# Normalised activations of the second row quarter: from a TensorE transpose to a DMA transpose, with a new instruction order

## The chip, the cores and the metric

The kernel runs on one core of a Trainium2 chip. The metric is the device time of one execution in microseconds (us). TensorE (PE) multiplies matrices, VectorE (DVE), ScalarE (ACT) and GpSimd (POOL) work on elements, SyncE (SP) mostly issues DMAs. DMAs stand in two queues here, one that SP feeds and one that ACT feeds; both are served by the same 16 DMA engines.

## The reference, cut to what matters

```python
xn = layernorm(A_q)                       # 2048 x 512
# branch A: a 4-tap shift, a long causal convolution by FFT, two gates
k_shift = sum over t of k_pad[:, t:t+S] * shift_k[:, 3-t]
kv = k_shift * v
y  = irfft(rfft(kv padded) * rfft(ssm_k padded)) + kv * ssm_D
s  = xn * y
# branch B: a gated MLP on the same normalised rows
h  = gelu(xn @ w_gate) * (xn @ w_up)      # 512 -> 1792, twice
g  = silu(h @ w_down)                     # 1792 -> 512
return A_q + s * g
```

## The kernel before, in words

**Branch B.** The 2048 rows are worked in four quarters q of 512 rows (four tiles of 128). For a quarter, `ln(q)` (L805) normalises rows of `X` into `XN` on DVE with one POOL instruction for the power of -1/2. `xn_transpose(q)` (L828) turns the four 128x512 tiles of `XN` into `xnT`, whose buffer has two halves, used by even and odd quarters. Then 14 calls of `unit(q, m)` (L1060) make the gate and up products of 128 columns each (4 matmuls `xnT,Wg` and 4 `xnT,Wu` of 128x512), gelu on ACT (`GE`) and the product on DVE (`HT`). `down(q)` (L1094) multiplies `HT` by `Wd`, 14 matmuls for each of four row tiles.

**Branch A.** The convolution is done as a two-stage transform by matrix products. The filter (`Hn`) is transposed on TensorE (L865) and goes through stage 1 (`HTr,F`), its results are stored to DRAM as `ZH` (8 stores from ACT's queue) and read back as `BH` for stage 2. The shifted and gated input (`kshift(i)`, L939, nine DVE instructions of 128x2048 for each quarter, written into `V`) goes through stage 1 (`V,F`, L900): for each u of 0 to 7 two products, each copied by ACT or DVE into a half of an `AST` or `ASX` slot, and then one SP store `ZK`. The `ZK` rows are read back as `BK`, multiplied by the filter's spectrum, transformed back (`ZI`, `BI`) and gated at the end.

**The four transposes before.** For quarters 0 and 1, `xn_transpose` puts 16 TensorE transposes of 128x128 (L841, in four groups of four) into PSUM banks and four copies to `xnT` (L846). For quarters 2 and 3 one DMA issued by SP (L833) transposes all 128x2048 elements from SBUF to SBUF; it stands in SP's queue with a length of 6.7 us in the plan.

**What sets the order.** `Sched.add` only records tasks. `Sched.run` (L344) walks the list `SEQ` (L27), a written-out order of all tasks by number (a `b` takes the task's second engine), gives each its engine and its buffers, and keeps a planned time for each from constants at L295 to L303. The instructions are then emitted in exactly this order, so each engine's stream, and each DMA queue, is the part of `SEQ` that falls to it, and each engine works its stream strictly in order. The planned times decide only which buffer slot a task takes. Loads of inputs are planned on an engine of their own name, "loads", but are issued by SP: on the chip they and SP's other DMAs are one stream. An instruction waits for semaphores: SP, too, stops at a DMA whose data is not ready, and everything behind it in its stream stops with it.

The plan charges a load its time in the table `LOAD_NS` and a fixed 2450 ns to land; a store that leaves before 46 us takes `TAKEN` from the loads:

```python
            if eng == "loads":
                free[eng] = t.start + dur * (self.EARLY[1] if t.start < self.EARLY[0] else 1.0)
                t.end = free[eng] + self.LOAD_LAT
            elif t.nbytes:
                en = t.end
                if en < self.SHARED:
                    free["loads"] += self.TAKEN
```

Of the kernel before, what the change touches and what calls it, by code (L numbers as in the profile page):

```python
# [19 lines left out]
NQ = 4  # L20
# [4 lines left out]
N_WARM = 14  # L25
ORDER = "x00 x01 w0 w1 h0 h1 h2 h3 D0 w2 s0 k0 v0 x1 w3 k1 v1 d0 d1 k2 v2 k3 v3 x2 x3"
SEQ = (  # L27
    "2 16 17 7 3 0 10 8 4 1 6 5 11 65 67 22 9 66 68 23 49 73 74 69 70 75 76 48 82 12 83 71 51 72 77 78 86b 53 55b 80 79 18 19 25 20 35 30 21 24 29 31 "
    "87 36 33 32 110 124 52 369 50 111 371 125 14 370 131 85 361 84 362 61 363 88b 364 372 89 132 60 373 112 365 375 113 37 63 62 367 374 366 13 447 "
    "449 451 445 450 446 368 452 448 376 453 454 15 457 455 377 133 381 134 383 379 54 385 378 389 139 141 138 140 391 57 382 380 384 456 59 56 126 "  # L30
    "390 386 387 58 127 392 458 95 96 388 97 421 98 413 135 114 142 415 115 460 414 143 144 422 27 28 26 38 34 423 416 405 128 459 424 145 146 150 64 "
    "147 99 136 137 129 393 461 395 462 401 409 394 465 130 463 407 464 466 411 116 396 403 148 410 402 105 412 397 119 151 404 152 107 106 417 418 "
    "419 117 420 108 118 495 406 121 120 122 153 408 154 149 398 471 90 497 399 91 92 491 93 492 100 493 101 102 400 155 494 499 496 217 42 40 158 "
    "473 94 501 109 218 103 500 425 467 39 44 45 43 41 156 498 159 502 472 219 474 160 157 511 222 475 123 104 469 220 221 476 161 513 477 223 478 "
    "162 224 435 232 436 225 233 468 234 227 235 228 437 229 479 426 163 166 164 167 470 168 165 169 230 481 438 427 430 431 440 441 242 428 81 432 "
    "429 170 171 439 226 182 172 47 244 231 174 236 177 46 176 243 237 433 245 442 483 238 173 239 484 485 240 443 486 487 246 175 241 489 252 253 "
    "254 512 434 444 634 514 247 249 480 255 515 248 256 636 482 635 250 178 516 517 179 251 507 508 503 180 543 638 640 637 639 641 518 642 643 547 "
    "509 187 183 184 544 545 646 645 644 546 510 548 504 519 185 521 505 181 257 647 520 488 490 188 189 190 549 538 539 523 258 550 283 259 270 186 "
    "192 506 551 522 262 524 528 525 552 271 526 272 556 554 553 260 555 261 263 275b 533 529 284 285 534 273 264 288b 527 535 648 265 191 266 296 "
    "530 540 531 268b 274 193 536 669 532 715 537 541 267 269 286 276 671 194 670 542 653 665 195 655 649 666 672 277 278 287 651 289 667 281 279 650 "  # L40
    "654 290 656 661 291 657 557 197 663 292 652 294b 668 658 297 610 298 301b 711 659 612 611 198 309 196 199 207 202 662 586 613 562 200 310 293 "
    "564 314 280 311 707 664 299 660 201 322 300 302 719 558 594 563 596 560 303 565 587 595 203 588 597 589 204 578 598 304 205b 580 305 559 579 590 "
    "581 312 561 307 600 206 323 582 282 592 308 306 327 324b 295 599 602 601 313 603 315 208 584 604 566 209 583 591 316 325 210 317 585 568 318 320 "
    "326 605 348 335 212 211 606 328 574 329 593 575 330 570 576 567 577 331b 569 333 336 571 337b 673 572 608 340 573 338 339 334 675 321 341 689 "
    "342 213 607 674 624 214 215 691 343 216 344 346 609 676 625 701 690 349 703 692 319 350 351 352 353 614 332 345 347 615 702 354 616 355 697 617 "
    "699 356 704 357 359b 358 619 626 698 360 627 705 713 700 618 620 629 709 681 621 622 683 682 623 628 684 677 693 630 631 679 678 706 680 723 708 "
    "770 742 714 685 632 695 687 694 710 732 729 725 716 696 712 733 686 735 633 734 774 772 736 730 721 688 743 722 717 731 724 778 727 744 718 737 "
    "726 745 738 746 720 728 749 750 780 751 756 752 747 776 757 739 753 758 775 773 763 740 759 764 754 765 760 761 766 779 771 748 781 777 741 767 "
    "755 768 762 769 "
)  # L50
NF_BANKS = 4
ISSUE = 470.0
# [239 lines left out]
class Sched:  # L292
# [7 lines left out]
    SHARE_BW = 300.0  # L300
    FIRST = {"loads": 300.0, "SP": 30500.0}
    DRAIN = 121.0
    EARLY, TAKEN, SHARED, WAIT = (2500.0, 1.6), 1700.0, 46000.0, 3300.0  # L303

    def __init__(self):
        self.tasks = []
# [87 lines left out]
def build_kernel(nc, A_q, A_k, A_v, A_shift_k, A_ssm_k, A_ssm_D, B_w_gate, B_w_up, B_w_down, out):  # L394
    with ExitStack() as es0:
# [20 lines left out]
        XN = new("XN", [128, NT, DM], BF16)  # L416
# [8 lines left out]
        ident = new("ident", [128, 128], BF16)  # L425
# [67 lines left out]
        S = Sched()  # L493
# [11 lines left out]
        def bank16(b):  # L505
            return PSB[:, 1024 * b.slot:1024 * (b.slot + 1)]

        def R_bank(b):
            return [R_ps[b.slot // 2][b.slot % 2]]
# [83 lines left out]
        def copy(e, h, o, i, scale=1.0):  # L593
            if e == "ACT":
                return h.activation(o, i, ACTF.Copy, scale=scale)  # L595
            if scale != 1.0:
                return h.tensor_scalar(o, i, scale, None, ALU.mult)
            return h.tensor_copy(o, i)
# [11 lines left out]
        bS = [B(f"S{j}") for j in range(8)]  # L610
        bst = [B(f"st{t}") for t in range(NT)]
        bmv = [[B(f"mv{q}_{h}") for h in range(2)] for q in range(NQ)]
        bxnT = [[B(f"xnT{q}_{h}") for h in range(1 if q > 1 else 4)] for q in range(NQ)]
        bF1, bG1, bMF, bMI, bid, bSKB = B("F1"), B("G1"), B("TF"), [B(f"MI{i}") for i in range(2)], B("id"), [B(f"SKB{j}") for j in range(4)]
        bHT = [[B(f"HT{q}_{m}") for m in range(MF)] for q in range(NQ)]
        bW = {n: [B(f"{n}{i}") for i in range(4)] for n in ("g", "u")}
# [188 lines left out]
        def ln(q):  # L805
            t_pws = []
            for t in range(4 * q, 4 * q + 4):
                t_stats[t] = op([("DVE", 670.0)], lambda e, h, t=t: h.bn_stats(stats[:, t, :], X[:, t, :]), r=[bX[q][t % 4]], w=[bst[t]], rr=[R_X[t]], ww=[R_st[t]])  # L808
                op([("DVE", 170.0)], lambda e, h, t=t: h.bn_aggr(mv[:, t, 0:2], stats[:, t, :]), r=[bst[t]], w=[bmv[q][t % 4 // 2]], rr=[R_st[t]], ww=[R_mv[t]])
            for h in range(1 if q else 2):  # L810
                n = 4 if q else 2
                ts = slice(4 * q + 2 * h, 4 * q + 2 * h + n)
                rm = R_mv[ts]
                bm = bmv[q] if q else [bmv[q][h]]
                be, b = B(f"var{q}_{h}"), B(f"rstd{q}_{h}")
                t_var = op([("DVE", 180.0)], lambda e, hd, ts=ts: hd.tensor_scalar(mv[:, ts, 2:3], mv[:, ts, 1:2], LN_EPS, None, ALU.add), r=bm, w=[be], rr=rm, ww=rm)  # L816
                t_pw = op([("POOL", 850.0)], lambda e, hd, ts=ts, n=n: hd.tensor_tensor(mv[:, ts, 3:4], mv[:, ts, 2:3], NHALF[:, 0:n, :], ALU.pow),  # L817
                          r=[bconst, be] + bm, w=[b], rr=rm + [R_nh], ww=rm)
                for t in range(ts.start, ts.stop):
                    op([("DVE", 420.0)], lambda e, hd, t=t: hd.tensor_scalar(XN[:, t, :], X[:, t, :], mv[:, t, 0:1], mv[:, t, 3:4], ALU.subtract, ALU.mult),  # L820
                       r=[bX[q][t % 4], b], w=[bXN[t]], rr=[R_X[t], R_mv[t]], ww=[R_XN[t]])
                t_pws.extend([t_var, t_pw])
            return t_pws

# [2 lines left out]

        def xn_transpose(q):  # L828
            af = gu_tasks[q - 2] if q >= 2 else (skb if q else [])
            if q > 1:  # L830
                def f(e):
                    o = xnT[:, q % 2, :, :, :].rearrange("k j d p -> k (j d) p")
                    trk.dma(e, lambda h: h.dma_start(out=o, in_=XN[:, 4 * q:4 * q + 4, :].rearrange("p t d -> p (t d)"), transpose=True), d_xt, r=R_XN[4 * q:4 * q + 4], w=R_xnT[q % 2])  # L833
                S.add([("SP", 6700.0)], f, r=bXN[4 * q:4 * q + 4], w=bxnT[q], nbytes=W_XT, after=af)
                return
            pp = [B(f"psxn{q}_{j}", pX) for j in range(4)]
            for j in range(4):
                def tr(e, j=j):
                    for kd in range(KD):
                        o = bank16(pp[j])[:, 128 * kd:128 * (kd + 1)]  # L840
                        trk.op("PE", lambda h, o=o, kd=kd: h.transpose(o, XN[:, 4 * q + j, 128 * kd:128 * (kd + 1)], ident[:]), r=[R_XN[4 * q + j], R_id], w=R_bank(pp[j]), accum=True)  # L841
                S.add([("PE", 4 * 66.0)], tr, r=[bid, bXN[4 * q + j]], w=[pp[j]], lat=200.0)
            for j in range(4):
                def ev(e, h, j=j):
                    return copy(e, h, xnT[:, q, j, :, :].rearrange("p k c -> p (k c)"), bank16(pp[j])[:, 0:512])
                xnT_tasks.append(op([("ACT", act(512)), ("DVE", dve(512, 2))], ev, r=[pp[j]], w=[bxnT[q][j]],  # L846
                   rr=lambda j=j: R_bank(pp[j]), ww=[R_xnT[q][j]], after=af))

        d_out = []
        gu_tasks = [[] for _ in range(NQ)]  # L850
# [387 lines left out]
```

## Time and profile before

| what | before |
|---|---|
| time, median of 3 (lowest to highest) | 196.93 us (196.27 to 197.09) |
| the profiled execution: its time, its span | 197.06 us, 195.3 us |
| around the span in that execution (the difference) | 1.8 us |
| granted TensorE clock | 1.000 |
| TensorE matmuls with 128x512 outputs on the whole array | 744 of 1396 |
| 32x32-tiled matmuls (L979), in 24 groups of 16 or 32 | 512 |
| DMA moved | 48.14 MB, mean 247 GB/s |

The span is the time from the first to the last instruction. Busy times are sums over one engine's instructions. The chain of waits goes back from the last instruction to what released it, again and again, so it shows what sets the end. A DMA has two times: how long its issue held the issuing engine, and the time from issue to landing.

### The profile page before, as it was taken

What the parts mean: (1) busy time and instruction counts of PE and PEld (TensorE: products, weight loads), DVE (VectorE), ACT (ScalarE), POOL (GpSimd) and SP (SyncE); (2) the same over time, 40 slices, a digit from 0 to 9 for tenths busy, and PEclk for the clock granted to TensorE, in tenths of its full rate; (3) what the DMA queues carried; (4) which work ended last, traced back from release to release, by engine and by line L of the source; (5) the groups of instructions that cost most, each with busy time, mean ns of one, the idle gap of its engine ahead of it and who ended that gap; (6) DMA issues with size and microseconds to landing.
All of it is one profiled execution on the core that took longest, in us unless ns stands there. A gap on an engine that the chain in (4) does not pass through costs nothing.

```text
span 195.3 us, 3519 instructions
## 1 busy us (share of the span) xinstructions
PE 190.4 (98%) x1396; PEld 87.4 (45%) x1396; DVE 156.4 (80%) x243; ACT 125.3 (64%) x172; POOL 11.4 (6%) x26
## 2 busy tenths in 40 slices
PE   7999999999999999999999999999999999999993
PEld 2695545444444444443344334343434444444442
DVE  5898899999899996967879689658884643399893
ACT  5679798589687888975558778686768452330111
POOL 7201700000000000022000000000000000000000
PEclk9999999999999999999999999999999999999999
DMA  5999999994828698599999607579532626568234
GB/s 160 359 330 344 361 386 395 415 401 175 351 120 300 232 283 276 215 301 311 318 263 311 225 2 263 170 246 321 191 107 111 215 85 232 223 193 274 110 146 139
DMA packets 34502, 48.14 MB, mean 247 GB/s; under 512 B 8499, under 2 KB 27191, under 8 KB 34486
## 3 DMA queue, kind: packets, MB, share of 16 engines
q1 hardware_dynamic: 28982, 39.53, 60.9%
q10 hardware_dynamic: 5504, 8.39, 11.5%
q8 instruction: 11, 0.18, 0.4%
q14 instruction: 5, 0.04, 0.1%
HBM read 27.39 MB, written 14.68 MB: 215 GB/s over the span
## 4 chain that ended last, share of the span: by engine, by line
PE 91%; DMA 6%; DVE 1%; SPq 0%; ACT 0%; issue 0%
PE psall L604 83%; PE psall L979 5%; DMA BI<-ZI 3%; DMA Hn<-in_A_ssm_k_dram 3%; PE psall L865 2%; PE psall L841 1%; SPq L576 0%; DVE G L1126 0%; DVE G L1125 0%; ACT G L1123 0%
## 5 line engine op out<-in xcount | busy, mean ns | idle before, releaser
L604 PE MATMUL psall<-xnT,Wg 128*128 128x512 bf16 (+1 forms) x232 | 56.1, 372 | 0.0
L604 PE MATMUL psall<-xnT,Wu 128*128 128x512 bf16 (+1 forms) x232 | 56.0, 372 | 0.0
L1091 DVE TENSOR_TENSOR HT<-psall,GE 128x512 bf16<-128x512 f32 x54 | 36.6, 684 | 20.8 <-PE psall L604 20.0
L604 PE MATMUL psall<-Wd,HT 128*128 128x512 bf16 (+2 forms) x238 | 52.7, 367 | 0.0
L1088 ACT ACTIVATE GE<-psall 128x512 bf16<-128x512 f32 x54 | 31.6, 601 | 14.7 <-PE psall L604 12.0
L604 PEld LDWEIGHTS psall<-Wd,HT 128*128 128x128 bf16 x238 | 22.1, 98 | 26.3 <-issue 2.3
L604 PEld LDWEIGHTS psall<-xnT,Wu 128*128 128x128 bf16 x232 | 22.0, 98 | 25.2 <-issue 1.1
L604 PEld LDWEIGHTS psall<-xnT,Wg 128*128 128x128 bf16 x232 | 21.8, 98 | 24.9 <-issue 1.3
L595 ACT ACTIVATE HS<-psall 128x1024 bf16<-128x1024 f32 x15 | 14.6, 1024 | 4.7 <-PE psall L979 4.7
L595 ACT ACTIVATE BO<-psall 128x1024 bf16<-128x1024 f32 x12 | 11.8, 1022 | 5.2 <-PE psall L979 5.0
L960 DVE TENSOR_TENSOR KTM<-KK,SKB 128x2048 bf16<-128x2048 bf16 x12 | 14.6, 1214 | 0.1
L962 DVE TENSOR_TENSOR KAC<-KAC,KTM 128x2048 bf16<-128x2048 bf16 x12 | 14.6, 1215 | 0.1
L1115 ACT ACTIVATE G<-psall 128x512 bf16<-128x512 f32 x12 | 7.1, 598 | 11.6 <-PE psall L604 11.6
L595 ACT ACTIVATE KB<-psall 128x1024 bf16<-128x1024 f32 x11 | 10.9, 1022 | 5.1 <-PE psall L979 4.8
L595 ACT ACTIVATE AST<-psall 128x1024 bf16<-128x1024 f32 x12 | 12.1, 1021 | 2.3 <-PE psall L604 2.1
L1042 DVE TENSOR_TENSOR HS<-KB,HS 128x1024 bf16<-128x1024 bf16 x16 | 10.9, 686 | 1.2 <-ACT KB L595 1.2
L1123 ACT ACTIVATE G<-psall 128x512 bf16<-128x512 f32 (+2 forms) x5 | 2.6, 512 | 14.2 <-PE psall L604 14.2
L1042 DVE TENSOR_TENSOR HW<-KB,HW 128x1024 bf16<-128x1024 bf16 x16 | 10.9, 685 | 0.0
L808 DVE BATCH_NORM_STATS2 stats<-X 128x6 f32<-128x512 bf16 x16 | 10.4, 680 | 0.5 <-DMA X<-in_A_q_dram 0.5
L1117 DVE SCALAR_TENSOR_TENSOR G<-G,psall 128x512 bf16<-128x512 bf16 x12 | 8.0, 681 | 3.2 <-ACT G L1115 3.2
L817 POOL TENSOR_TENSOR mv<-mv,NHALF 128x4 f32<-128x4 f32 (+1 forms) x5 | 5.4, 1072 | 78.8 <-DVE mv L816 78.8
L595 ACT ACTIVATE XN<-psall 128x1024 bf16<-128x1024 f32 (+1 forms) x10 | 8.6, 859 | 1.3 <-PE psall L604 1.1
(79 smaller groups left out, 177.9 us busy)
## 6 DMA issues: line engine op xcount, KB each, us to landing
BH<-ZH SPq DMA_DIRECT2D x8, 512.0 KB, 4.5
HW<-HS SPq DMA_DIRECT2D x16, 256.0 KB, 3.1
BK<-ZK SPq DMA_DIRECT2D x8, 512.0 KB, 5.6
ZI<-BO ACTq DMA_DIRECT2D x16, 256.0 KB, 3.3
BI<-ZI SPq DMA_DIRECT2D x8, 512.0 KB, 5.0
ZK<-AST SPq DMA_DIRECT2D x6, 512.0 KB, 2.9
Hn<-in_A_ssm_k_dram SPq DMA_DIRECT2D x4, 512.0 KB, 7.1
KK<-in_A_k_dram SPq DMA_DIRECT2D x4, 512.0 KB, 11.8
```

The costliest lines, as they stand in the source:

```text
L595: return h.activation(o, i, ACTF.Copy, scale=scale)
L604: return h.matmul(o, lhsT=l, rhs=r, start=st, stop=sp)
L808: t_stats[t] = op([("DVE", 670.0)], lambda e, h, t=t: h.bn_stats(stats[:, t, :], X[:, t, :]), r=[bX[q][t % 4]], w=[bst[t]], rr=[R_X[t]], w ...
L817: t_pw = op([("POOL", 850.0)], lambda e, hd, ts=ts, n=n: hd.tensor_tensor(mv[:, ts, 3:4], mv[:, ts, 2:3], NHALF[:, 0:n, :], ALU.pow), r=[b ...
L960: op([("DVE", dur)], lambda e, h, j=j, m=m: h.tensor_tensor(KTM[:, m.slot, :, :], kk(j), sk(j), ALU.mult), r=need + [bSKB[j], a], w=[m], r ...
L962: op([("DVE", dur)], lambda e, h, m=m: h.tensor_tensor(KAC[:, a.slot, :, :], KAC[:, a.slot, :, :], KTM[:, m.slot, :, :], ALU.add), r=[m], ...
L979: trk.op("PE", lambda h: h.matmul(ps(s, i)[b, :], lhsT=wt(col)[a, :], rhs=data(col)[a, :], start=n < 16, stop=n >= len(todo) - 16, tile_po ...
L1042: return hd.tensor_tensor(o, flat(KB, kb[h]), o, ALU.mult)
L1088: op([("ACT", act(512))], lambda e, h: h.activation(GE[:, g.slot, :], bank(pg), ACTF.Gelu_apprx_tanh), r=[pg], w=[g], rr=lambda: R_bank(pg ...
L1091: op([("DVE", dve(512, 1))], lambda e, h: h.tensor_tensor(HT[:, q % 2, m, :], bank(pu), GE[:, g.slot, :], ALU.mult), r=[pu, g], w=[bHT[q][m]],
L1115: op([("ACT", act(n))], lambda e, h, g=g, pc=pc: h.activation(g, pc(), ACTF.Tanh, scale=0.5), r=[p], w=[bt], rr=lambda p=p: R_bank(p), ww= ...
L1117: op([("DVE", dve(512, 1))], lambda e, h, g=g, pc=pc: h.scalar_tensor_tensor(out=g, in0=g, scalar=1.0, in1=pc(), op0=ALU.add, op1=ALU.mult ...
```

## The change

`xn_transpose(1)` becomes a DMA transpose like those of quarters 2 and 3. Its 16 TensorE transposes and four copies are gone. Its task is planned on "loads" with 400 ns, behind every load, and is emitted on SP; the normed tiles of quarter 1 count as ready 5 us later than planned before. A store that leaves early is charged 1500 ns of the loads' time in place of 1700. `SEQ` is a new order of all tasks, 775 in place of 782. `XN` of quarter 1 has one reader fewer on TensorE, and `bxnT[1]` is one buffer for all four tiles.

```diff
 SEQ = (
-    "2 16 17 7 3 0 10 8 4 1 6 5 11 65 67 22 9 66 68 23 49 73 74 69 70 75 76 48 82 12 83 71 51 72 77 78 86b 53 55b 80 79 18 19 25 20 35 30 21 24 29 31 "
...
+    "0 2 3 4 7 10 16 11 17 8 65 1 5 6 67 66 69 68 22 49 70 73 74 71 48 9 72 23 12 19 18 76 51 77 75 24 35 83 87 78 53 13 20 30 82 131 52 124 110 86b "
...
-    EARLY, TAKEN, SHARED, WAIT = (2500.0, 1.6), 1700.0, 46000.0, 3300.0
+    EARLY, TAKEN, SHARED, WAIT = (2500.0, 1.6), 1500.0, 46000.0, 3300.0
...
-        bxnT = [[B(f"xnT{q}_{h}") for h in range(1 if q > 1 else 4)] for q in range(NQ)]
+        bxnT = [[B(f"xnT{q}_{h}") for h in range(1 if q else 4)] for q in range(NQ)]
...
-                       r=[bX[q][t % 4], b], w=[bXN[t]], rr=[R_X[t], R_mv[t]], ww=[R_XN[t]])
+                       r=[bX[q][t % 4], b], w=[bXN[t]], rr=[R_X[t], R_mv[t]], ww=[R_XN[t]], lat=5000.0 if q == 1 else 0.0)
...
-            if q > 1:
+            if q:
                 def f(e):
                     o = xnT[:, q % 2, :, :, :].rearrange("k j d p -> k (j d) p")
-                    trk.dma(e, lambda h: h.dma_start(out=o, in_=XN[:, 4 * q:4 * q + 4, :].rearrange("p t d -> p (t d)"), transpose=True), d_xt, r=R_XN[4 * q:4 * q + 4], w=R_xnT[q % 2])
-                S.add([("SP", 6700.0)], f, r=bXN[4 * q:4 * q + 4], w=bxnT[q], nbytes=W_XT, after=af)
+                    trk.dma("SP", lambda h: h.dma_start(out=o, in_=XN[:, 4 * q:4 * q + 4, :].rearrange("p t d -> p (t d)"), transpose=True), d_xt, r=R_XN[4 * q:4 * q + 4], w=R_xnT[q % 2])
+                S.add([("SP", 6700.0)] if q > 1 else [("loads", 400.0)], f, r=bXN[4 * q:4 * q + 4], w=bxnT[q], nbytes=W_XT, after=af + ([t for t in S.tasks if t.opts[0][0] == "loads"] if q == 1 else []))
                 return
```

The built programs show where the new order puts things. On TensorE, all units of quarter 0, 42 of its 56 down products, all of the filter's stage 1 and 16 of the 32 `V,F` products now stand ahead of the first product of quarter 1. In SP's stream the DMA transpose of quarter 1 stands behind all 30 load DMAs and behind one more DMA, the first `ZK` store, which waits for an ACT copy. On ACT, two of the `ZH` stores stand behind the copy that releases this `ZK` store. On TensorE the first filter transposes now have four `XN` transposes between them in place of eight, and the load of quarter 1's `X` stands ahead of the second pair of `Wg`, `Wu` pieces in place of between them.

## The prediction

> **What bounds the kernel now.** I read the page first: busy times, then the chain of waits by share.
>
> ```profile
> span 195.3 us, 3519 instructions
> ...
> PE 190.4 (98%) x1396; PEld 87.4 (45%) x1396; DVE 156.4 (80%) x243; ACT 125.3 (64%) x172; POOL 11.4 (6%) x26
> ...
> PEclk9999999999999999999999999999999999999999
> ...
> PE 91%; DMA 6%; DVE 1%; SPq 0%; ACT 0%; issue 0%
> ```
>
> TensorE is busy for 98% of the span at full granted clock, and 91% of the chain is TensorE. Of its 4.9 us of idle time, 4.7 lie ahead of the first transposes (1.17 + 0.44) and behind the end of the last product at 192.1 (3.1). So there are two rules for any edit: a TensorE instruction taken away is worth its slot, and a wait put in front of a TensorE instruction costs its whole length, for there is no idle time later in which it could be made up. What other engines lose or win counts only through such a wait.
>
> Next, the chain in order of time gives the slots of the four removed groups of transposes.
>
> ```profile
> 27.26 0.22 PE psall L841 x4
> ...
> 30.51 0.22 PE psall L841 x4
> 30.73 0.86 PE psall L604 x4
> 31.59 0.45 PE psall L841 x8
> 32.04 48.35 PE psall L604 x226
> ```
>
> They are on the path, 0.22, 0.22 and 0.45 us. The last line gives the price of a product: 226 in 48.35 us, 0.214 us (four in 0.86: 0.216; I use 0.216).
>
> Third, the DMA transposes that are there already: the list of DMA issues, and SP's stream.
>
> ```profile
> ZK<-AST SPq DMA_DIRECT2D x6, 512.0 KB, 2.9
> ...
> xnT<-XN SPq DMA_TRANSPOSE x2, 7.6
> ...
> MI<-TFA SPq DMA_TRANSPOSE x1, 3.1
> ```
> ```profile
> 63.87 0.32 SPq L576 DMA_DIRECT2D ZK<-AST  x1
> 64.23 1.92 SPq L990 DMA_TRANSPOSE G<-F  x1
> ...
> 89.29 6.14 SPq L833 DMA_TRANSPOSE xnT<-XN  x1
> ...
> 97.44 3.59 SPq L833 DMA_TRANSPOSE xnT<-XN  x1
> ```
>
> The two of the same form (128x2048) landed 8.1 and 7.1 us after their issue. One of half the size, with little beside it (`MI<-TFA`), took 3.1 us.
>
> **The change part by part.**
>
> *Removed.* 16 transposes, 0.22 + 0.22 + 0.45 = 0.89 us of TensorE. The four copies (0.6 us each on ACT) go too; ACT is 64% busy and off the chain, so nothing is gained there.
>
> *Kept.* The other matmuls are the same in number and form, and the 32x32 products still stand in 24 groups, so the cost of changing between forms is unchanged. This cover is exact: it follows from the order of the built program.
>
> *The wait on the DMA transpose.* Quarter 1's normed rows are ready early (normed at 20.8 to 24.6 us before the change), and the loads were all in by 47 us, so the data does not decide. SP's stream does: the transpose stands behind the first `ZK` store, and that waits for ACT's copy of the second `V,F` product pair. I count from the end of this pair's TensorE slots, E. From the rows of the same step before the change: the pair `V,F` started at 53.03 us, so its slots ended at 53.46; ACT's copy ran from 53.66 for 1.02, and the store was issued at 54.72: E + 1.26. In the new order another ACT copy stands just ahead, worth about 0.1. From the `ZK` line to the next transpose line above is 0.36. So the transpose is issued at E + 1.7. On TensorE, 31 products of 0.216 stand between E and the first product of quarter 1: it is wanted at E + 6.7. A landing within 5.0 us of the issue costs nothing, and every 0.1 us beyond costs 0.1 us.
>
> How long does it take? Bounds from both sides. Low: `MI<-TFA` took 3.1, and 128 KB stores to `out` landed in 1.7, so of the 3.1 some 1.5 are for moving 256 KB; 512 KB alone would be about 1.6 + 3.0 = 4.6 us, an estimate from these rows: no wait. High: 8.1, the slower of the two like it: a wait of 3.1. What stands beside it in the new order: the `ZK` store just ahead (512 KB, 2.6 alone, issued 0.4 us earlier, so up to 0.6 of its move is in the way), and two `ZH` stores of 512 KB on ACT's queue, issued about 1.3 and 3.5 us after the transpose (behind two ACT copies more, of 1.0 and 0.6 us, and behind another two of 1.0), some 1.0 to 1.3 of moving each. That `ZH` stores and SP's transfers share one capacity shows in the trace: beside the loads they landed in 6.5 to 8.4 us, alone in 2.6. So 4.6 + 0.6 + 1.0 = 6.2 with one store in the way, 7.2 to 7.8 with both. I take 7.1, the row that had one read just ahead of it and two stores beside it (`ZI`, from ACT's queue): a wait of 2.1 us, with 0 and 3.1 kept for the range. Behind the waiting product on TensorE stands all that is left: the other engines drain and wait too.
>
> SP is held 3.6 to 6.1 us by the issue. Behind it stand the second `ZK` store and the first read of `ZH`; the read is wanted by TensorE over 15 us later, and the store's slot is written again 13 ACT instructions later, so I cost this at nothing; without that cover it would cost up to those 6.1 us.
>
> The skill has a rule against my reading. The Trainium skill, "Advanced Engine Details and Errata", section X-Bar Transpose (TRN2), says that transpose DMAs are as fast as regular ones. By it the 512 KB would land like a `ZK` store, in 2.9 us, and the sum would be without the wait. The trace disagrees at half the size: 3.1 us for 256 KB transposed, 2.6 for 512 KB stored.
>
> *The start.* Before, eight `XN` transposes hid the wait for the second `Hn` piece: the first eight filter transposes end at 8.25, `XN` at 8.70, the piece lands at 8.66. Now only four stand there (0.22): TensorE is ready at 8.47 and waits 0.23. Second, DVE:
>
> ```profile
> 15.19 2.47 DVE L808 BATCH_NORM_STATS2 stats<-X 128x6 f32<-128x512 bf16 x4 [0.49 <-DMA X<-in_A_q_dram]
> ```
>
> DVE waited for `X` of quarter 1 with its `HT` products of that time already done. Now two statistics stand ahead of two `HT` products that free PSUM banks for TensorE. `X` follows the third `Hn` piece (11.6 us) and took 1.5 to 2.1 more: 13.1 to 13.7. Two statistics at 0.59 and one `HT` of 0.42 give 14.7 to 15.4; TensorE, by the slots from 8.70 on, is at that product at 14.8. So 0 to 0.6 us; I take 0.3.
>
> *The rest.* From quarter 1 on the order is new, but TensorE had hardly a wait in it before, and the reads it needs stand as far ahead as before. I cost it at nothing, with 0.3 either way for the last `BI` reads, one of which landed just as TensorE came to it.
>
> *Sum.* 197.06 (this execution's own time) - 0.89 + 0.23 + 0.3 + 2.1 = 198.8. The median of the shown times is 0.13 lower, so 198.7.
>
> **The rivals.**
>
> *Hidden after all* (not slower): the transpose lands within 5.0 us, because one or both `ZH` stores miss it. Then 197.06 - 0.89 + 0.53 = 196.7, and 196.4 if `X` is early too. For it: the lone estimate of 4.6 and the page's rule. Against: both rows of its size, and the two stores in its window. It decides at 5.0 us from issue to landing.
>
> *Longer*: landing at 8.1 or later, as in the first row, with the late `X`: 197.06 - 0.89 + 0.23 + 0.55 + 3.1 = 200.1. For it: the transpose moves in packets under 512 bytes (8499 such are listed) beside stores in larger ones. Against: in the 8.1 us row several reads and swaps stood ahead in SP's queue.
>
> *It does not do what it says*: "behind all loads" is what the plan has; the stream puts it behind a store too, and that wait is in no term of the plan, which books 0.4 us and 2.45 to land. Ahead of that store it would go out when the loads end (47 us) and be hidden: again 196.7. The order of the built program excludes this, so it gets no chance of its own.
>
> **How the numbers follow.** Forecast (a wait of 1.4 to 3.0 us) 0.61, hidden or nearly so 0.26, longer 0.13. A measurement of this kernel tells about 0.5% from no change, that is below 195.95 or above 197.91. The first and the last are slower; 0.23 of the hidden case is within 0.5%, and 0.03 is left for faster, which would need the whole 0.89 and something more. The range goes from 196.3 (hidden, `X` early, on the median) to 200.7 (longer, with 0.6 for a transpose slower than either row).
>
> **What would show it.** Right: the chain after the change holds `DMA xnT<-XN` once, 1.4 to 3 us long, at 56 to 59 us, directly ahead of the first product of quarter 1; the waits list TensorE (or its weight load) on that DMA; SP's line of the transpose comes 0.4 us behind the first `ZK` line; TensorE's busy time is about 0.9 lower. Small waits stand near 8.5 (`Hn`) and 15 us (`HT`). Wrong: no such wait (then the DMA took under 5 us), or an issue well before the first `ZK` store, or waits of TensorE behind 60 us, which I have costed at nothing.

## The result, and the profile after

| | before | after |
|---|---|---|
| time, median (lowest to highest), same chip | 196.36 us (196.17 to 197.09) | 201.63 us (200.92 to 203.25) |
| profiled execution: time, span | 197.06, 195.3 | 201.31, 199.5 |
| granted TensorE clock | 1.000 | 0.991 |

The change makes the kernel slower: ratio 1.0265, 95% interval 1.0228 to 1.0303. 198.7 was predicted, 196.3 to 200.7 as range; the sign was right, the size was not.

The page of the changed kernel, with the same lines as shown of before:

```profile
span 199.5 us, 3479 instructions
...
PE 189.2 (95%) x1367; PEld 86.7 (43%) x1380; DVE 159.6 (80%) x244; ACT 122.5 (61%) x167; POOL 12.6 (6%) x26
...
PE   7899999999929999999999999999999999999993
...
PEclk9999999999997999999999999999999999999999
...
PE 86%; DMA 7%; ACT 2%; issue 1%; DVE 1%; POOL 1%; SPq 1%; DVEq 0%
```

TensorE has one hole, slice 12 of 40 (55 to 60 us), and in the slice right behind it the granted clock reads 0.7. Both are new. The chain in order of time (start, length, what) shows what ends the hole:

```profile
48.91 1.03 ACT AST L594
...
49.95 0.33 SPq L575
50.28 0.04 issue
50.33 8.92 DMA xnT<-XN
59.25 0.14 issue
59.38 12.12 PE psall L603 x48
```

ACT's copy releases the first `ZK` store, SP issues it and then the transpose, and the transpose lands 8.92 us later. The two `ZH` stores leave 0.9 and 1.8 us behind it on ACT's queue (their timeline):

```profile
51.23 0.33 ACTq L575 DMA_DIRECT2D ZH<-X  x1
52.09 0.33 ACTq L575 DMA_DIRECT2D ZH<-XN  x1
```

The last line of the chain holds the second loss: 48 products in 12.12 us are 0.253 us each, not 0.216. Cut into stretches of 1 us (columns: busy time with count of PE, PEld, DVE, ACT, POOL; then PEclk, DMA share, GB/s):

```profile
59.00:60.00 1.00, 0.62 (x2) 0.28 (x3) 0.00 (x0) 0.00 (x0) 0.00 (x0) 0.62 0.65 266
60.00:61.00 1.00, 1.00 (x3) 0.29 (x2) 0.00 (x0) 0.00 (x0) 0.00 (x0) 0.50 0.44 94
61.00:62.00 1.00, 1.00 (x4) 0.39 (x3) 0.00 (x0) 0.71 (x2) 0.00 (x0) 0.50 0.71 164
62.00:63.00 1.00, 1.00 (x5) 0.36 (x4) 0.02 (x1) 0.97 (x2) 0.00 (x0) 0.67 1.10 408
63.00:64.00 1.00, 1.00 (x6) 0.42 (x5) 1.00 (x2) 0.98 (x2) 0.00 (x0) 1.00 1.00 391
```

The clock is at half from about 59.24 to 62.66 (0.38 + 0.50 + 0.50 + 0.33 = 1.71 us of lost full-speed time, so 3.42 us at half). TensorE's rows show the products in it:

```profile
54.69 0.81 PE L603 MATMUL psall<-V,F 128*128 128x512 bf16 x3
59.38 1.86 PE L603 MATMUL psall<-xnT,Wg 128*128 128x512 bf16 x4 [3.88 <-DMA xnT<-XN]
61.05 1.83 PE L603 MATMUL psall<-xnT,Wu 128*128 128x512 bf16 x4
62.71 1.03 PE L603 MATMUL psall<-xnT,Wg 128*128 128x512 bf16 x4
```

Eight products take from 59.38 to 62.71, 3.33 us instead of 8 x 0.216 = 1.73: 1.60 lost.

**The account.** From the first filter transpose to the end of the last product on the chain, before took 7.26 to 191.36 and after 6.93 to 195.60: 184.10 and 188.67, 4.57 more. The transposes gone give -0.89, the wait +3.88, the slow products +1.60: 4.59. The 3.88 is idle time as the profile counts it, from the modelled end of the last product (55.50). Counted from the end of that product's slot (54.69 + 3 x 0.216 = 55.34), the next one starts 4.04 us late, and the sum is 4.75. So to within 0.2 us nothing is left for the rest of the order. (The start itself came 0.33 earlier, with the first `Hn` piece.)

### The profile page after: what moved, and what is told of

It reads as the page before. It is cut to its first block, busy times and chain, and to the rows that moved or that the text cites. A ratio compares the mean times of both kernels' runs of the same rounds, so it can differ in the third digit from the quotient of the medians.

```text
span 199.5 us, 3479 instructions
## 1 busy us (share of the span) xinstructions
PE 189.2 (95%) x1367; PEld 86.7 (43%) x1380; DVE 159.6 (80%) x244; ACT 122.5 (61%) x167; POOL 12.6 (6%) x26
## 4 chain that ended last, share of the span: by engine, by line
PE 86%; DMA 7%; ACT 2%; issue 1%; DVE 1%; POOL 1%; SPq 1%; DVEq 0%
PE psall L603 78%; PE psall L978 5%; DMA xnT<-XN 4%; DMA Hn<-in_A_ssm_k_dram 3%; PE psall L864 2%; POOL mv L816 1%; SPq L575 1%; ACT AST L594 1%; ACT HTr L594 0%; PE psall L840 0%; DVE HT L1080 0%; ACT GE L1078 0%; DVE G L1125 0%; DVE G L1124 0%; ACT G L1122 0%
## 5 line engine op out<-in xcount | busy, mean ns | idle before, releaser
L603 PE MATMUL psall<-Wd,HT 128*128 128x512 bf16 (+2 forms) x230 | 51.4, 366 | 0.9 <-issue 0.8
L594 ACT ACTIVATE HS<-psall 128x1024 bf16<-128x1024 f32 x16 | 15.6, 1023 | 5.5 <-PE psall L978 5.5
L594 ACT ACTIVATE BO<-psall 128x1024 bf16<-128x1024 f32 x10 | 10.0, 1023 | 5.4 <-PE psall L978 5.3
L594 ACT ACTIVATE KB<-psall 128x1024 bf16<-128x1024 f32 x10 | 10.1, 1022 | 4.3 <-PE psall L978 4.3
L816 POOL TENSOR_TENSOR mv<-mv,NHALF 128x4 f32<-128x4 f32 (+1 forms) x5 | 6.6, 1321 | 80.8 <-DVE mv L815 80.8
L597 DVE CAST KB<-psall 128x1024 bf16<-128x1024 f32 x6 | 7.3, 1224 | 5.4 <-PE psall L978 5.4
L594 ACT ACTIVATE AST<-psall 128x1024 bf16<-128x1024 f32 x10 | 10.1, 1024 | 2.1 <-PE psall L603 2.1
```

Source lines behind the costliest of these rows:

```text
L603: return h.matmul(o, lhsT=l, rhs=r, start=st, stop=sp)
```

## The experiments

The theory: the loss is the wait on the landing, made long by the two `ZH` stores beside the transpose, and the half clock that the idle time brings. The rivals: the new order costs by itself; the transpose is slow by itself; the clock falls for another cause. Times are medians. The ratios are against the kernel before as it ran beside each experiment: 196.66 us for e1_first, e2_zh_late, e3_te and e5_fill16, 196.70 for e4_one_late, e5_fill8 and e8_first_late, 196.86 for e5_fill4 and e6_later.

**The order alone (e3_te).** The new order with quarter 1's 16 transposes and four copies back, as in the code before; the transposes ran between 30.4 and 35 us. In the new order's list the numbers above 459 go up by 7, the transpose's 459 goes, and 459 463, 460 464b, 461 465, 462 466b (one group of transposes and its copy each, `b` for DVE) come in. The changed lines of code go back as well; one of them:

```diff
-            if q:
+            if q > 1:
```

> The new order of the changed kernel, with quarter 1 transposed on TensorE again (16 transposes and four copies, two on ACT and two on DVE, put in between 24 and 36 us). It undoes the transpose alone. Theory (the order costs nothing by itself): 196.2 to 196.9, the 0.89 us of transposes back and the wait gone. Rival (a good part of the loss lies in the new order): 198 or more.

Measured: 196.48 (195.95 to 196.81), ratio 0.9988, interval 0.9965 to 1.0011. The order costs nothing that can be measured; the whole loss lies in the DMA transpose and what it brings.

**The two stores out of its way (e2_zh_late).** Tasks 109 and 123 are the two `ZH` stores:

```diff
-223 459 429 160 224 232 433 109 225 233 123 441 161 434 227 442 228 162 166 163 234 235 229 464
+223 459 429 160 224 232 433 225 233 441 161 434 227 442 228 162 166 163 234 235 109 123 229 464
```

> The changed kernel with the two ZH stores that stood beside the transpose moved on ACT's queue, behind the last copy of the V,F products ahead of quarter 1 (issue near 56 us instead of 51.2 and 52.1). The transpose keeps its place behind the first ZK store. Theory (the two stores take 3 to 4 of the 8.9 us): it lands 5 to 5.5 us after its issue, TensorE waits 0 to 0.4 us, no fall of the clock: 195.8 to 196.6. Rival (the transpose is slow by itself, 256-byte packets): landing still after 8 us or more, time still 200.5 to 201.6.

Measured: 195.66 (195.20 to 196.47), ratio 0.9957, interval 0.9935 to 0.9979: faster than either kernel. SP's timeline gives the issue, 49.59:

```profile
49.21 0.33 SPq L575 DMA_DIRECT2D ZK<-AST  x1
49.59 3.33 SPq L832 DMA_TRANSPOSE xnT<-XN  x1
```

It landed 5.09 us later, at 54.68; the two stores left at 54.37 and 54.73. The waits have no `xnT` any more, the clock is 1.000. But it landed with nothing to spare. The chain of that time:

```profile
53.95 0.81 PE psall L603 x3
...
54.82 7.28 PE psall L603 x33
```

The slots of the three products end at 54.60 (53.95 + 3 x 0.216), and the next product starts 0.22 later, 0.14 behind the landing, as the waiting products of the changed kernel and of e4_one_late do (0.13 and 0.14). Against e3_te, which has the same order and TensorE transposes, this kernel is 0.82 us faster, close to the 0.89 of the prediction.

**One store out of its way (e4_one_late).** Only 123 moved.

> The changed kernel with only the second of the two ZH stores beside the transpose moved behind the last copies ahead of quarter 1 on ACT; the first stays. Theory (each store costs the transpose 1.9 us): landing 7.0 us after its issue, a wait of 1.8, no fall of the clock: 197.2 to 197.8. Rival (1.0 to 1.3 us per store, the prediction's figure): landing 6.2, a wait of 1.0: 196.4 to 196.9. Rival (the second store alone does the harm, being the one that lands just ahead of the transpose): landing 5.1 to 5.5, 195.6 to 196.1.

Measured: landing after 6.71 us, TensorE waits 1.68, clock 1.000, 197.41 (197.11 to 197.82), ratio 1.0033, interval 1.0012 to 1.0053. So the landing is 5.09, 6.71, 8.92 us with none, one and two 512 KB stores left in their place: 1.6 and 2.2 us for each, not 1.0 to 1.3. (The moved store left at 54.98, and 0.2 MB of it had gone out when the transpose landed at 56.91, so "one" is a little more than one here.)

**The transpose by itself (m1_alone).**

```python
            for n in STEPS:
                if 0 in stores[n]:
                    store(e, n, 0)
                if n != "G":
                    transpose(e, n, half=n == "B")
                    e.wait_ge(d_t[n], 16)
```

> A program of its own that computes nothing of the reference: it loads 1 MB, runs DMA transposes and 512 KB stores in steps with a wait between them, and copies rows to the output. Measured is the time from issue to landing of a 128x2048 transpose: TRA alone; TRB a half (128x1024) alone; TRC behind one store on SP's queue; TRD beside one store on ACT's queue issued 0.6 to 0.9 us later; TRE beside two of them; TRF behind one and beside two, as in the changed kernel; and one store alone (ZG). Theory (the transpose's packets and the stores share one capacity, and each 512 KB store costs it 1.9 us): TRA 4.2 to 4.7, TRB about 3.1, TRC 5.1, TRD 6.2 to 6.6, TRE 8 to 8.5, TRF 8.5 to 9. Rival (slow by itself): TRA above 6. Second rival (stores cost it only their own 1.0 to 1.3 us): TRE 6.6 to 7.2. ZG 2.6.

Its list of DMA issues (last column: us to landing):

```profile
ZGX<-ST SPq DMA_DIRECT2D x1, 512.0 KB, 2.6
TRA<-XN SPq DMA_TRANSPOSE x1, 4.3
...
TRC<-XN SPq DMA_TRANSPOSE x1, 5.1
TRD<-XN SPq DMA_TRANSPOSE x1, 4.7
TRE<-XN SPq DMA_TRANSPOSE x1, 7.7
TRF<-XN SPq DMA_TRANSPOSE x1, 9.4
```

Alone 4.3 (half of it 3.0), behind one store 5.1, beside two 7.7, behind one and beside two 9.4; each was measured once. It is not slow by itself as the rival had it, but it takes 4.3 us where a store of as many bytes takes 2.6. Beside two stores it lies between the theory's 8 to 8.5 and the second rival's 6.6 to 7.2, and with all three it lies above the theory's 8.5 to 9. The store ahead costs 0.8 us with nothing beside, 1.7 with two beside, so the prices do not simply add up. (In step D the store left 2.1 us behind the transpose, later than meant, so 4.7 says little.)

**Ahead of the first `ZK` store (e1_first, e8_first_late).** Task 459 moved directly behind the last load:

```diff
-92 39 91 44 43 45 93
+92 39 91 44 43 45 459 93
...
-220 221 223 459 429
+220 221 223 429
```

> The changed kernel with one task of the order moved: quarter 1's DMA transpose stands directly behind the last load in SP's stream, ahead of every wait of SP and of the first ZK store. Theory (the loss is the wait of TensorE on this transpose, 3.9 us, and 1.6 us of half-speed products behind it, and nothing else): the transpose is issued near 35.7 us, lands by 50, both costs go, and what is left is the 0.89 us of transposes saved: 195.4 to 196.2 us against about 196.4 for the kernel before. Rival (the new order costs something by itself): the wait goes, yet the time stays above 197. Second rival (the 256-byte packets disturb the loads and stores of 36 to 50 us): TensorE waits for V or for a PSUM bank at 45 to 56 us, 197 to 199.

Measured: the profiled execution took 195.68 us, without a wait; issue 34.35, SP held for 12.4 us, landing only at 53.46, for the loads are ahead of it and two `ZH` stores beside it. But five of its twelve times were 200.30 to 201.95 at a clock of 0.991 or 0.983 and the other seven 195.68 to 197.33; the ratio, 0.9981 (0.9949 to 1.0014), is that of the seven. Only four of the twelve lie in the expected 195.4 to 196.2. The landing has only 1.9 us to spare there. So it was run again with the stores moved as in e2_zh_late:

> Both moves at once: the transpose directly behind the last load, and the two ZH stores behind the last copies ahead of quarter 1. With the first move alone five of twelve times were 200.3 to 201.95 us at a granted clock of 0.991 or 0.983, the others 195.68 to 197.33 at 0.998 to 1.000. Theory (there the transpose now and then lands 4 us or more later, held up by the ZH and ZK stores, and TensorE waits for it): with the stores away the times are all 195.2 to 196.6. Rival (a transpose queued behind loads is late now and then by itself): the two groups of times stay.

Measured: 196.33 (195.79 to 198.41), ratio 0.9977, interval 0.9942 to 1.0012; all ten at a clock of 0.998 or above. The group above 200 is gone, as the theory has it, but four of the ten lie above the expected 196.6, and the spread is 2.6 us against 1.3 for e2_zh_late; why is not known. No profile of a time above 200 was taken, so that the landing is late in them is inferred from the clock and from this run, not seen.

**Filling the wait (e5_fill16, e5_fill8, e5_fill4).** Products without use ahead of quarter 1's first, so that the idle time gets shorter while the landing stays:

```diff
                 def f(e):
+                    if (q, m, nm) == (1, 1, "g"):
+                        for i in range(16):
+                            trk.op("PE", lambda h: mm(h, bank(p), W[:, 0, 0:128], xnT[:, 0, :, 0, :], True, True), r=[R_Wc[nm, 0], *R_xnT[0]], w=R_bank(p), accum=True)
                     for kd in range(KD):
```

> The changed kernel with 16 idle products (a weight and rows of quarter 0 that are there long before, into the bank that the first product of quarter 1 overwrites) directly ahead of the first product of quarter 1: 3.5 us of TensorE work within the 3.9 us of waiting. They add nothing to the output. Theory (the idle time takes the clock down, and that costs 1.6 us behind the wait): the wait shrinks to 0.4, the clock stays at 1.00, and the time falls by 1.6: 199.8 to 200.2. Rival (the clock fall has another cause, or the slow products are hidden by later slack): 201.3 to 201.9, as the changed kernel.

> The changed kernel with 8 idle products instead of 16 ahead of the first product of quarter 1, so that about 2.1 us of the waiting stay idle. The landing is as in the changed kernel. Theory (the clock falls only when the idle time is longer than a threshold between 2.1 and 3.9 us): clock 1.00, 199.4 to 200.0, as with 16. Rival (the loss behind the wait grows with the idle time): 0.9 us lost, 200.3 to 200.9.

> The changed kernel with 4 idle products ahead of the first product of quarter 1, so that 3.0 to 3.3 us of the waiting stay idle; 2.4 us of idle time left the clock at 1.00, 3.9 us took it to half speed. Theory (a threshold, a little under the 3.9 us): one side or the other for all times of the kernel or a mixture of both, nothing between: 199.4 to 200.0 at a clock of 1.00, or 201.2 to 201.8 at 0.991. Rival (a loss that grows with the idle time): about 200.8 at 0.995.

| products put in | idle time in the profile | clock of each time | time, median (lowest to highest) |
|---|---|---|---|
| 0 (the changed kernel) | 3.88 | 0.983 to 0.991 | 201.63 (200.92 to 203.25) |
| 4 | 2.85 | 0.991, 1.000, 0.991, 0.991 | 200.75 (199.58 to 201.26) |
| 8 | 2.38 | 1.000, 0.998, 0.999, 1.000 | 199.66 (199.31 to 201.09) |
| 16 | under 0.5 | 1.000 in all four | 199.52 (199.34 to 199.72) |

16 useless products make the kernel 2.1 us faster (2.4 by the ratios to the kernel before, 1.0265 and 1.0143). Between the two profiled executions it is 1.97 (201.31 and 199.34), of which 0.32 is an earlier landing (58.93); the other 1.65 agrees with what the half clock cost. The profiles with 8 and with 4:

```profile
59.58 1.04 PE L603 MATMUL psall<-xnT,Wg 128*128 128x512 bf16 x4 [2.38 <-DMA xnT<-XN]
```
```profile
58.90 1.43 PE L603 MATMUL psall<-xnT,Wg 128*128 128x512 bf16 x4 [2.85 <-DMA xnT<-XN]
60.12 1.91 PE L603 MATMUL psall<-xnT,Wu 128*128 128x512 bf16 x4
61.82 1.53 PE L603 MATMUL psall<-xnT,Wg 128*128 128x512 bf16 x4
```

With 8, four products take 0.88 (to 60.46), full speed. With 4, twelve take 58.90 to 63.19, 4.29 us instead of 2.59: 1.70 lost, about as much as behind 3.88 us of idle time. So the loss behind the wait comes whole or not at all; it does not grow with the idle time. Of the three times with 4 products at 0.991, two (200.58 and 200.91) lie below the expected 201.2 to 201.8, and the median alone would fit the rival's 200.8. In the profile the landing was 0.4 us earlier than in the changed kernel (58.85), and the 1.70 and the clock of 0.991 speak against the rival. The 201.09 with 8 products, at a clock of 0.998, is not explained.

How much idle time it takes is not read from the length of the wait alone. In the clock records of the three profiles with a fall (the changed kernel, 4 products, e6_later) the half clock lasts 3.413 us and the full clock ahead of it 54.613, 16 times as long; the full-clock records of the profiles without a fall are whole multiples too (191.146 in e2_zh_late, 56 times). So the clock changes on a grid of 3.413 us. In the step that ends where the half clock begins, TensorE was idle throughout in the changed kernel (55.83 to 59.25), for 2.85 us with 4 products (step 56.00 to 59.41) and for 2.77 in e6_later (56.92 to 60.34). With 8 products the grid, counted on from the start of the record at 3.94, has a step's end at 58.56, which cuts the 2.38 us of idle time into 1.36 and 1.02: no fall. So it goes by the idle time within one step: 2.77 us was enough, 1.36 was not, and what lies between was not measured. The grid lies differently in each profile, which may be why one time with 4 products kept its clock.

**A later issue (e6_later).** The second `ZK` store put ahead of the transpose.

```diff
-220 221 223 459 429 160 224 232 433 109 225 233
+220 221 223 429 160 224 232 433 109 225 226 459 233
...
-462 230 226 177
+462 230 177
```

> The changed kernel with the second ZK store moved ahead of the transpose in SP's stream, which delays its issue to about 55.0 us. Theory (the wait is issue plus landing less the time at which the product is wanted; the clock's loss is a fixed 1.6 to 1.8 us however long the idle time): beside the later part of the second ZH store it lands after 6 to 7 us, near 61.5, TensorE idles 5.5 to 6.5 us, and the time is 203 to 204.2 at a clock of 0.991. Rival (the clock's loss grows in proportion to the idle time, 0.41 us for each): 2.3 to 2.7 us of loss, 204 to 205.1 and a clock of 0.987. Second rival (the landing goes by the stores alone, and the later issue ends at the same 59.3): 201.3 to 201.9.

Measured: 201.84 (201.51 to 202.73), clock 0.991 or 0.992. The theory's number fell, the second rival's held. SP's timeline:

```profile
50.16 3.13 SPq L575 DMA_DIRECT2D ZK<-AST  x2
53.33 4.42 SPq L832 DMA_TRANSPOSE xnT<-XN  x1
```

Issued 3.0 us later than in the changed kernel, with the second `ZK` store ahead of it, the transpose landed at 59.56, 0.3 later; TensorE waited 3.99. So "issue plus a fixed landing time" is not how it goes. The bytes say more: from the issue of the first `ZK` store to the landing, 2.47 MB were moved in 9.30 us in the changed kernel and 2.68 MB in 9.40 us here. Of the second `ZK` store some 0.4 MB had been moved by the landing in the changed kernel too, although SP issued it behind the transpose, so putting it ahead added only 0.2 MB. The half clock again cost 1.7 (PEclk 0.67, 0.50, 0.50, 0.62 in the four stretches from 60 us).

## Why the prediction was wrong, point by point

*The bound, and the 16 transposes at 0.89*: right (0.82 between e2_zh_late and e3_te, with 0.22 of waiting still in e2_zh_late).

*Issue and slack*: right. The transpose was issued at 50.33, 0.38 behind the `ZK` line, and wanted at 55.34, when the slots ahead of its product end: 5.0 us of slack, as worked out. Holding SP for 3.92 us cost nothing, as forecast: TensorE waited for nothing that stood behind it.

*The landing: the failing step, "I take 7.1, the row that had one read just ahead of it and two stores beside it".* It took 8.92, so the wait is 3.88 (4.04 by the slots, as the prediction counts) instead of 2.1. The row was misread. In the trace of before its two stores stand on ACT's queue so:

```profile
102.94 1.00 ACTq L576 DMA_DIRECT2D ZI<-BO  x2
```

That is 5.5 us behind the issue of that transpose (97.44), they move 256 KB each, not 512, and they landed at 108, when it had landed at 104.57. Up to then the DMA list has no packet on ACT's queue, so they were not in its way at all. The 1.4 MB that were moved beside that transpose belong to other DMAs of SP's queue, issued ahead of it and, at 101.07 and 101.70, behind it. The prediction's own sum from parts, 7.2 to 7.8, was the better figure, and was passed over for a row that only looked alike. Its parts, measured one at a time: 4.6 alone (measured 4.3), 0.6 for the `ZK` store ahead (0.75, from 4.32 to 5.07), and 1.0 to 1.3 for each `ZH` store (1.6 and 2.2). Only the last was too small: it is the store's own moving time, and the transpose loses more than that. The two were expected 1.3 and 3.5 us behind the transpose and left 0.9 and 1.8 behind it; so both were fully in its way and landed before it (55.96 and 59.06).

*The clock: a term that the sum did not have.* The prediction read "full granted clock" as given. The wait of 3.88 took it away, and that is another 1.60. Whether the forecast 2.1 us would have left the clock alone is not shown (1.68 did, and 2.38 cut by a step's end). This is also why the range missed: its upper end had a wait of 3.1 to 3.7 without the price that comes with it. Half speed for 3.42 us behind 3.88 of idle time, the same length in two other kernels. The Trainium skill, "TensorE: Matmul & The Clock Gate", Part 1, What's actually happening, has that rule: half rate after an idle window of about 3.4 us, full rate again after a busy window as long, the windows running freely. The trace agrees with the length and with a grid that runs on its own. A window that counts as idle need not be idle throughout: 2.77 and 2.85 of 3.41 us were enough.

*The start at 0.23 + 0.3*: wrong, it cost nothing. The chain of the changed kernel runs through it without a gap:

```profile
6.93 1.16 PE psall L864 x8
8.09 0.22 PE psall L840 x4
8.31 0.66 PE psall L864 x4
```

The second `Hn` piece landed at 8.21, 0.1 before TensorE was ready for it (8.66 before the change, from another execution). For the `HT` copies TensorE was never idle between 10 and 20 us by more than 0.05.

*The rest at nothing, within 0.3*: right (e3_te).

*"Ahead of that store ... again 196.7"*: tried in e1_first. It was hidden in the profiled execution and, by the times, in seven of twelve.

*The rival "Longer", 200.1*: nearest to the result, and its condition, a landing at 8.1 or later, came true. That its number is so near is partly luck: it holds 0.78 for the start, which cost nothing, and lacks the 1.60 of the clock. What spoke for it, small packets beside large ones, is not shown to be the reason, for no run changed the size of the packets.

*The rule of the Trainium skill, "Advanced Engine Details and Errata", X-Bar Transpose (TRN2), that transpose DMAs are as fast as regular ones*: the trace disagrees, 4.3 against 2.6 us for 512 KB, each alone. By the rule there would have been no wait at all; yet even 1.7 us off the 8.92 would have left one of about 2.2 (an estimate from these rows).

## What to carry to other kernels

Price a DMA's landing by what is moved until it ends, on all queues and in bytes, what was issued shortly behind it included; and before a row is taken as the likeness, look when its neighbours were issued, how large they are and whether they landed before it. This is a rough price: from issue to landing of this transpose the DMA engines moved 255 to 281 GB/s in e2_zh_late, e4_one_late, the changed kernel and e6_later (1.30 to 2.47 MB), but 204 and 223 in steps E and F of m1_alone (TRE and TRF). A wait put in front of a busy TensorE costs its length, and another 1.7 us for the clock once enough of it (2.8 us was, 1.4 was not) falls into one step of the clock's grid. So a forecast of such a wait has a step in it, with both outcomes near it. Where a wait on one transfer is the whole loss, moving the transfers beside it may do more than moving the transfer: two stores of other data, issued some 3.5 us later, turned 2.7% slower into 0.4% faster, though with no time to spare.

## What the runs showed of the hardware that was not expected

- The half clock begins at the end of a step of 3.41 us and lasts one step, wherever the products start again: 0.1 us before them in the changed kernel, 0.5 behind them with 4 products put in, 0.6 in e6_later.
- One time of the changed kernel (203.25) and one of e1_first had a clock of 0.983; 0.017 x 201 us is 3.4 us, which would be two falls of 1.7. Neither was profiled, so the second fall is not shown.
- A transpose issued 3 us later, behind the second `ZK` store, landed 0.3 us later (e6_later). How the engines share packets between the two queues was not measured, and why two stores cost it 3.8 us in all stays open.
- A transpose that SP issues while loads are queued holds SP for 12.4 us (e1_first), against 3.3 to 4.4 for the same transpose where the loads are in.
